# Window attention on one core: VectorE's exponential as a product of factors read from PSUM, GpSimd ungated, lead-in padded

## The chip, the cores and the metric

The kernel runs on one core of one Trainium2 chip. The metric is device time in microseconds (us) of one execution. The profile's span of the same execution is 1.8 us shorter (1096.08 against 1094.3 for the kernel before), so times are compared with times and spans with spans. Five engines count here. TensorE ("PE" in the profile, its weight loads "PEld") multiplies. ScalarE (ACT) takes exponentials out of PSUM, the accumulator memory. VectorE (DVE) does arithmetic and moves results from PSUM to SBUF. GpSimd (POOL) helps with arithmetic, from SBUF alone. SyncE (SP) issues transfers.

## The reference

Cross-shaped window attention on a 224 x 224 image with 96 channels in bfloat16. Half of the channels attend inside horizontal stripes 8 rows high, half inside vertical stripes 8 columns wide. Each stripe has 1,792 positions, and there are 28 of each kind.

```python
qkv = jnp.einsum('bhwc,cd->bhwd', x, wqkv)
q, k, v = qkv[..., :C], qkv[..., C:2 * C], qkv[..., 2 * C:]
scale = C2 ** (-0.5)                                   # C2 = 48
qh = q[..., :C2].reshape(B * nh, sw * W, C2)           # 28 stripes, 1792 positions
... # kh, vh the same
ah = _softmax(jnp.einsum('bqc,bkc->bqk', qh, kh) * scale, axis=-1)
oh = jnp.einsum('bqk,bkc->bqc', ah, vh).reshape(B, H, W, C2)
... # qv, kv, vv, av, ov: the same with vertical stripes and the other 48 channels
return jnp.einsum('bhwc,cd->bhwd', o, wo)
```

The heavy part is the exponential: 56 stripes x 1,792 x 1,792 scores. The kernel cuts them into 1,372 tiles of 128 x 1024.

## The kernel before

The kernel is a program that *plans*: while it emits instructions it keeps a clock of its own for each engine (`now`, `tfree`), with an assumed duration for every instruction, and always gives the next instruction to the engine that would be free. On the chip each engine then runs its fixed list in order, held by semaphores. So a change of one duration or one constant reorders everything that follows it. A score tile goes one of three ways.

On ScalarE, one instruction, assumed to occupy it for 917 ns and to finish after 1277:

```python
e = add("act", [ev, bufA_ev[sl]], lambda e, base=base, sl=sl: e.activation(
    PTA[sl][:], ps[:, base * 512:(base + 2) * 512], ACTF.Exp, scale=LN2 / 128.0), 917.0, 1277.0)
```

On VectorE, by arithmetic: the scores are scaled so that the number, rounded to a 16-bit integer, is nearly the bit pattern of the bfloat16 exponential. What is missing is a correction that depends on the fraction of the exponent, and this fraction can be read as the low half of the 32-bit word. A cubic in it is computed in five passes, the middle three from SBUF to SBUF in 16 bits:

```python
D_OCC = [t_ps(1024), 0.521 * 1024 + 75, 0.26 * 1024 + 75, 0.521 * 1024 + 75, t_ps(1024)]

def d_step(k, sl):
    if k == 0:
        return lambda e: e.tensor_scalar(tt_sb[:], dps.bitcast(U16)[:, 0:2048:2], CS / 65536.0, CS * CA3, ALU.mult, ALU.add)
    if k == 1:
        return lambda e: e.tensor_tensor(sq_sb[:], tt_sb[:], tt_sb[:], ALU.mult)
    if k == 2:
        return lambda e: e.tensor_scalar(sq_sb[:], sq_sb[:], CB, None, ALU.add)
    if k == 3:
        return lambda e: e.tensor_tensor(tt_sb[:], sq_sb[:], tt_sb[:], ALU.mult)
    return lambda e: e.scalar_tensor_tensor(PTD[sl][:].bitcast(U16), dps, CC, tt_sb[:], ALU.add, ALU.add)
```

On GpSimd, after VectorE has copied the tile to SBUF (`zp_sb`), by six operations of the same arithmetic. Each carries a gate, a wait for the instruction that VectorE issued last, and is planned only where VectorE is about to read PSUM; it may be cut into halves of 512 to fit:

```python
gate = (s_dve, cnt["dve"] - 1, 0.0)
c0, c1 = 512 * pick[0], 512 * pick[1]
ev = add("pool", ws + [gate], lambda e: p_step(e, k, zi, sl, c0, c1), p_dur(k, n))
```

The lead-in is written by hand: the first key and query projections, four padding matmuls, the first score tiles, then further projections ("fills"). Transposed input is loaded and results are stored through SyncE's queue.

The softmax here doesn't subtract the row's maximum and nothing guards it: scores larger than these inputs give would overflow.

## Time and profile before

| | before |
|---|---|
| time, median of the first 3 runs | 1095.41 us (1094.14 to 1096.42) |
| span of the profiled run | 1094.3 us, granted TensorE clock 0.993 |
| score tiles on ScalarE / VectorE / GpSimd | 1169 / 158 / 45 |
| busy: ScalarE / VectorE / TensorE / GpSimd | 98% / 96% / 95% / 53% |
| first exponential on ScalarE begins / last one ends | 8.40 / 1088.24 us |

How to read it: all tiles need an exponential, ScalarE takes most of them, and it is hardly ever idle. So the time is the number of ScalarE's tiles times its pace, plus a start, gaps and a tail. The lines are shown in the prediction.

### The profile page before, as it was taken

The numbers are of one execution on the slowest core, as the hardware profiler recorded it, in microseconds if no ns is written. First come the engines' busy times: TensorE is split into PE (matmuls) and PEld (weight loads), VectorE is DVE, ScalarE is ACT, GpSimd is POOL, SyncE is SP. The second block draws the span as 40 slices with busy tenths as digits, with TensorE's granted clock in tenths as the row PEclk, the third lists the DMA queues.
The fourth block names the chain that finished last, engine by engine and source line by source line (L and its number), as shares of the span: only waits on it lengthen the run. The fifth ranks groups of instructions, "written<-read, shape, count | busy, mean of one in ns | idle before, by whom it ended". The sixth has DMA issues, their size and how long they took to land.

```text
span 1094.3 us, 28704 instructions
## 1 busy us (share of the span) xinstructions
PE 1040.7 (95%) x12104; PEld 372.7 (34%) x12104; DVE 1047.4 (96%) x1712; ACT 1077.2 (98%) x1172; POOL 584.6 (53%) x451
## 2 busy tenths in 40 slices
PE   9999999999999999999999999999999999999997
PEld 2333333332333333233333333333333333333332
DVE  5999999999999999999999999999999999999996
ACT  6999999999999999999999999999999999999997
POOL 0544555453545645364564465656565565656563
PEclk7999999999999999999999999999999999999999
DMA  5301001101110120110111122122222222221111
GB/s 99 69 9 35 19 18 36 36 10 27 36 27 10 35 36 7 30 35 17 20 35 27 35 44 41 39 41 42 41 41 40 39 42 41 39 41 38 24 28 37
DMA packets 169001, 37.37 MB, mean 34 GB/s; under 512 B 168872, under 2 KB 168872, under 8 KB 168872
## 3 DMA queue, kind: packets, MB, share of 16 engines
q1 hardware_dynamic: 167256, 35.35, 17.3%
q8 instruction: 94, 1.54, 0.6%
q10 hardware_dynamic: 1616, 0.18, 0.1%
q14 instruction: 35, 0.29, 0.1%
HBM read 0.15 MB, written 9.63 MB: 9 GB/s over the span
## 4 chain that ended last, share of the span: by engine, by line
ACT 71%; DVE 21%; PE 4%; POOL 1%; issue 1%; DMA 0%; SPq 0%; DVEq 0%; POOLq 0%
ACT PTA L892 71%; DVE tt_sb L903 4%; DVE PTD L910 3%; DVE sq_sb L905 2%; DVE tt_sb L909 2%; PE ps L194 2%; PE ps L853 1%; DVE sq_sb L907 1%; DVE KT_sb L522 1%; DVE zp_sb L1056 1%; DVE tmp L624 1%; DVE OT_sb L937 1%; DVE V_sb L431 1%; POOL PTP L985 1%; DVE QT_sb L498 1%
## 5 line engine op out<-in xcount | busy, mean ns | idle before, releaser
L892 ACT ACTIVATE PTA<-ps 128x1024 bf16<-128x1024 f32 x1169 | 1075.0, 1214 | 5.9 <-PE ps L194 5.1
L194 PE MATMUL ps<-QT_sb,KT_sb 49*64 49x512 bf16 (+3 forms) x5488 | 486.5, 369 | 38.9 <-ACT PTA L892 25.5
L853 PE MATMUL ps<-PTA,V_sb 128*64 128x512 bf16 (+1 forms) x2674 | 422.9, 367 | 0.6 <-DVE Ph_sb L584 0.2
L190 PEld LDWEIGHTS <-KT_sb 49*64 49x64 bf16 (+1 forms) x5488 | 137.4, 103 | 335.0 <-issue 321.9
L903 DVE TENSOR_SCALAR tt_sb<-ps 128x1024 f16<-128x1024 uint16 x158 | 192.9, 1221 | 11.6 <-PE ps L194 7.1
L910 DVE SCALAR_TENSOR_TENSOR PTD<-ps,tt_sb 128x1024 uint16<-128x1024 f32 x158 | 192.5, 1219 | 1.3
L853 PEld LDWEIGHTS ps<-PTA,V_sb 128*64 128x64 bf16 x2674 | 119.8, 108 | 204.1 <-issue 162.8
L647 POOL TENSOR_TENSOR out_sb<-tmp,Ph_sb 128x480 bf16<-128x480 f32 (+2 forms) x89 | 105.6, 1195 | 110.9 <-DVE sq_sb L907 57.9
L978 POOL TENSOR_TENSOR uq_sb<-up_sb 128x1024 f16<-128x1024 f16 (+1 forms) x52 | 101.3, 1952 | 111.6 <-DVE sq_sb L907 57.5
L982 POOL TENSOR_TENSOR up_sb<-uq_sb,up_sb 128x512 f16<-128x512 f16 (+1 forms) x65 | 112.3, 1732 | 84.8 <-DVE sq_sb L907 27.4
L984 POOL TENSOR_TENSOR zp_sb<-zp_sb,up_sb 128x512 f32<-128x512 f32 (+1 forms) x74 | 111.2, 1508 | 54.6 <-DVE sq_sb L907 31.7
L976 POOL TENSOR_SCALAR up_sb<-zp_sb 128x1024 f16<-128x1024 uint16 x45 | 47.1, 1047 | 130.3 <-DVE zp_sb L1056 115.4
L905 DVE TENSOR_TENSOR sq_sb<-tt_sb 128x1024 f16<-128x1024 f16 x158 | 113.1, 716 | 0.1
L909 DVE TENSOR_TENSOR tt_sb<-sq_sb,tt_sb 128x1024 f16<-128x1024 f16 x158 | 109.9, 696 | 2.9
L462 PE MATMUL ps<-xT_sb,w_sb 128*64 128x448 bf16 (+3 forms) x448 | 85.7, 380 | 6.1 <-DVE KT_sb L522 3.0
L937 DVE CAST OT_sb<-ps 128x512 bf16<-128x512 f32 (+5 forms) x118 | 69.3, 591 | 1.4 <-PE ps L853 1.4
L907 DVE TENSOR_SCALAR sq_sb<-sq_sb 128x1024 f16<-128x1024 f16 x158 | 68.2, 432 | 2.2
L1056 DVE COPY zp_sb<-ps 128x1024 f32<-128x1024 f32 x45 | 55.0, 1222 | 8.8 <-POOL PTP L985 4.6
L853 PE MATMUL ps<-PTD,V_sb 128*64 128x512 bf16 (+1 forms) x360 | 62.1, 362 | 0.0
L985 POOL TENSOR_SCALAR PTP<-zp_sb 128x512 uint16<-128x512 f32 (+1 forms) x66 | 57.4, 870 | 5.7 <-POOL zp_sb L984 0.2
L624 DVE TENSOR_TENSOR tmp<-ps,rc 128x480 f32<-128x480 f32 (+2 forms) x92 | 53.2, 578 | 1.1
L522 DVE TENSOR_TENSOR KT_sb<-ps,shift 128x448 bf16<-128x448 f32 (+2 forms) x84 | 51.6, 615 | 2.1 <-PE ps L462 2.1
(55 smaller groups left out, 668.3 us busy)
## 6 DMA issues: line engine op xcount, KB each, us to landing
out_dram<-out_sb SPq DMA_DIRECT2D x389, 24.0 KB, 1.9
xT_sb<-in_x_dram SPq DMA_TRANSPOSE x332, 2.6
w_sb<-in_wqkv_dram ACTq DMA_DIRECT2D x2, 54.0 KB, 3.1
out_dram<-out_sb ACTq DMA_DIRECT2D x3, 24.0 KB, 1.9
wo_sb<-in_wo_dram SPq DMA_DIRECT2D x4, 9.0 KB
wo_sb<-one_sb SPq DMA_DIRECT2D x4, 0.0 KB
```

Source lines behind the costliest of these rows:

```text
L190: return e.add_instruction(mybir.InstLdweights(tile_size=(64, 64), tile_position=pos, name=nc.get_next_instruction_name(), engine=mybir.En ...
L194: return e.add_instruction(mybir.InstMatmult(start_tensor_calc=True, stop_tensor_calc=True, tile_size=(64, 64), tile_position=pos, ldweigh ...
L647: return e.tensor_tensor(out_sb[b][:, wdw, k0:k0 + n, :], tmpi[:, 0:n, :], Ph_sb[:, k0:k0 + n, j, :], ALU.add)
L853: ins = e.matmul(bk[64 * wdw:64 * wdw + 64, 0:qs], lhsT=V_sb[b][:, wdw, kt, :], rhs=pt[:, wdw * 512 + i * qs:wdw * 512 + (i + 1) * qs], st ...
L892: e = add("act", [ev, bufA_ev[sl]], lambda e, base=base, sl=sl: e.activation(PTA[sl][:], ps[:, base * 512:(base + 2) * 512], ACTF.Exp, sca ...
L903: return lambda e: e.tensor_scalar(tt_sb[:], dps.bitcast(U16)[:, 0:2048:2], CS / 65536.0, CS * CA3, ALU.mult, ALU.add)
L905: return lambda e: e.tensor_tensor(sq_sb[:], tt_sb[:], tt_sb[:], ALU.mult)
L909: return lambda e: e.tensor_tensor(tt_sb[:], sq_sb[:], tt_sb[:], ALU.mult)
L910: return lambda e: e.scalar_tensor_tensor(PTD[sl][:].bitcast(U16), dps, CC, tt_sb[:], ALU.add, ALU.add)
L978: return e.tensor_tensor(q, u, u, ALU.mult)
L982: return e.tensor_tensor(u, q, u, ALU.mult)
L984: return e.tensor_tensor(z, z, u, ALU.add)
```

## The change

Its intent is to give ScalarE fewer tiles by using GpSimd's idle half. VectorE's correction is rewritten as a product of three linear factors of the fraction, each read from PSUM anew, so that no pass of it should need the SBUF ports that VectorE shares with GpSimd. GpSimd then needs no gates and no halves, and takes 94 tiles. The key projection's shift loses its SBUF pass in the same manner. The lead-in gets eight more padding matmuls, against the fall of TensorE's clock. The planner's constants are chosen anew.

```diff
-CS, CA3, CB, CC = 2.153502696265075, 0.9658066371188914, -31.056571874438696, 55.5867689628946
+CD, CA, CB = 9.864582734494235, 2.9538561147169977, -3.956077288180509
+PS, PA, PB, PC = 2.153502696265075, 0.9658066371188914, -31.056571874438696, 55.5867689628946
 ... (NZP 1 -> 2, SLACK 120 -> 160, LOOK 8 -> 7, HOLD 0 -> 110, ENDD, PADA = 5, PADB = 1, and other planner constants)
-        D_OCC = [t_ps(1024), 0.521 * 1024 + 75, 0.26 * 1024 + 75, 0.521 * 1024 + 75, t_ps(1024)]
+        D_OCC = [t_ps(1024)] * 4
+        HA = CA / 2
+        RT = (HA * HA - CB) ** 0.5
         def d_step(k, sl):
+            frac = dps.bitcast(U16)[:, 0:2048:2]
             if k == 0:
-                return lambda e: e.tensor_scalar(tt_sb[:], dps.bitcast(U16)[:, 0:2048:2], CS / 65536.0, CS * CA3, ALU.mult, ALU.add)
+                return lambda e: e.tensor_scalar(tt_sb[:], frac, (HA + RT) * U, CD / U ** 3, ALU.add, ALU.mult)
             if k == 1:
-                return lambda e: e.tensor_tensor(sq_sb[:], tt_sb[:], tt_sb[:], ALU.mult)
+                return lambda e: e.scalar_tensor_tensor(sq_sb[:], frac, (HA - RT) * U, tt_sb[:], ALU.add, ALU.mult)
             if k == 2:
-                return lambda e: e.tensor_scalar(sq_sb[:], sq_sb[:], CB, None, ALU.add)
-            if k == 3:
-                return lambda e: e.tensor_tensor(tt_sb[:], sq_sb[:], tt_sb[:], ALU.mult)
-            return lambda e: e.scalar_tensor_tensor(PTD[sl][:].bitcast(U16), dps, CC, tt_sb[:], ALU.add, ALU.add)
+                return lambda e: e.tensor_tensor(tt_sb[:], sq_sb[:], frac, ALU.mult)
+            return lambda e: e.tensor_tensor(PTD[sl][:].bitcast(U16), tt_sb[:], dps, ALU.add)
 ... (GpSimd: whole tiles, no safe(), no gate)
-                ev = add("pool", ws + [gate], lambda e: p_step(e, k, zi, sl, c0, c1), p_dur(k, n))
+                ev = add("pool", ws, lambda e: p_step(e, k, zi, sl), p_dur(k))
 ... (K's shift: the SBUF pass becomes a second pass from PSUM)
 ... (lead-in)
+        pad(PADA)
         early_qk(2)
+        for f in [pf0["K"][1], pf0["V"][0]]:
+            f.run_now()
+        early_qk(3)
         for f in [pf0["V"][1], pf0["K"][2]]:
             f.run_now()
-        early_qk(3)
+        pad(PADB)
+        early_qk(4)
         for f in [pf0["V"][2], pf0["K"][3]]:
             f.run_now()
+            pad(PADB)
```

## The prediction

> **What bounds the kernel now.** I read the page first, then the waits of ScalarE, then the timelines of the start, the middle and the end. Every one of the 1,372 score tiles (128x1024) needs an exponential. Part 5 of the page tells who computes it: 1,169 on ScalarE (line 892), 158 on VectorE (one pass each of lines 903, 905, 907, 909, 910), 45 copied out by VectorE (line 1056) and computed on GpSimd (lines 976 to 985); 1169 + 158 + 45 = 1372.
>
> ```profile
> PE 1040.7 (95%) x12104; PEld 372.7 (34%) x12104; DVE 1047.4 (96%) x1712; ACT 1077.2 (98%) x1172; POOL 584.6 (53%) x451
> L892 ACT ACTIVATE PTA<-ps 128x1024 bf16<-128x1024 f32 x1169 | 1075.0, 1214 | 5.9 <-PE ps L194 5.1
> L903 DVE TENSOR_SCALAR tt_sb<-ps 128x1024 f16<-128x1024 uint16 x158 | 192.9, 1221 | 11.6 <-PE ps L194 7.1
> L905 DVE TENSOR_TENSOR sq_sb<-tt_sb 128x1024 f16<-128x1024 f16 x158 | 113.1, 716 | 0.1
> L909 DVE TENSOR_TENSOR tt_sb<-sq_sb,tt_sb 128x1024 f16<-128x1024 f16 x158 | 109.9, 696 | 2.9
> L907 DVE TENSOR_SCALAR sq_sb<-sq_sb 128x1024 f16<-128x1024 f16 x158 | 68.2, 432 | 2.2
> ```
>
> ScalarE's exponentials overlap (1214 ns each by record), so their cost is the busy time over the count, 1075.0 / 1169 = 0.920 us. The reader should see the idle time in the second line: 5.9 us in the whole run. The timeline of ScalarE says where it lies.
>
> ```profile
> 8.40 1.94 ACT L892 ACTIVATE PTA<-ps 128x1024 bf16<-128x1024 f32 x2 [1.03 <-PE ps L194]
> ...
> 16.88 1.02 ACT L892 ACTIVATE PTA<-ps 128x1024 bf16<-128x1024 f32 x1 [0.54 <-PE ps L194]
> 18.44 1.02 ACT L892 ACTIVATE PTA<-ps 128x1024 bf16<-128x1024 f32 x1 [0.54 <-PE ps L194]
> 20.00 1.02 ACT L892 ACTIVATE PTA<-ps 128x1024 bf16<-128x1024 f32 x1 [0.54 <-PE ps L194]
> ...
> 99.46 973.82 ACT L892 ACTIVATE PTA<-ps 128x1024 bf16<-128x1024 f32 x1059
> ```
>
> From 24.4 us on ScalarE is without a gap, but for one of 0.18 us: 1,059 exponentials run as one block. So the span is: start to first exponential, 8.4; 1169 x 0.920 = 1075; gaps after the first exponential, 4.9 - of which the nine between 8.4 and 24.4 us sum to 3.9; and the tail after the last exponential (end at 1077.10 + 11.14 = 1088.24) of 6.1. That makes 1094.4 against a span of 1094.3. ScalarE is the bound; VectorE at 96% is almost one, and GpSimd has 47% idle.
>
> The nine early gaps have one cause. The windows view shows TensorE's clock falling to half at 11 us and staying there until 24:
>
> ```profile
> 10.00:11.00 1.00, 1.00 (x26) 0.69 (x23) 1.00 (x2) 0.69 (x2) 0.00 (x0) 1.00 0.35 54
> 11.00:12.00 1.00, 1.00 (x10) 0.27 (x9) 1.00 (x3) 0.69 (x2) 0.00 (x0) 0.54 0.45 92
> ...
> 22.00:24.00 2.00, 2.00 (x14) 0.44 (x12) 1.68 (x3) 1.39 (x2) 0.00 (x0) 0.50 0.54 104
> 24.00:26.00 2.00, 2.00 (x26) 0.64 (x22) 0.86 (x5) 1.53 (x2) 0.00 (x0) 0.82 0.49 83
> ```
>
> (Length, then busy time and count of PE, PEld, DVE, ACT, POOL, then the clock.) The score matmuls then come too late, and a lone exponential costs 1.02 instead of 0.92.
>
> **Why GpSimd is half idle.** Its timeline beside VectorE's:
>
> ```profile
> 337.58 2.44 POOL L982 TENSOR_TENSOR up_sb<-uq_sb,up_sb 128x1024 f16<-128x1024 f16 x1 [2.97 <-DVE QT_sb L494]
> 337.35 0.68 DVE L909 TENSOR_TENSOR tt_sb<-sq_sb,tt_sb 128x1024 f16<-128x1024 f16 x1
> ...
> 678.48 2.13 POOL L984 TENSOR_TENSOR zp_sb<-zp_sb,up_sb 128x1024 f32<-128x1024 f32 x1
> ```
>
> The bracket is the gate that the kernel puts on GpSimd: it may start only where VectorE is about to make a PSUM pass. Even so it was 0.45 us late at the end of VectorE's pass 909, and the operation reads 2.44. I laid each full-width two-input operation of GpSimd over VectorE's passes: those that begin 0.45 us before the end of a pass 909 are 0.31 longer than clean ones, those 0.58 before it are 0.44 longer, and 2.43 - 0.31, 2.56 - 0.44 and the clean 2.12 of line 984 agree. The square of line 978 (same operand twice) gives 2.20 - 0.31 = 2.33 - 0.44 = 1.89. One-input operations are 1.05 always.
>
> **What the Trainium skill says.** "SBUF — State Buffer", section "SBUF: two separate sides": VectorE and GpSimd share a port pair, held exclusively for a whole instruction by whichever starts first, on VectorE's side by passes in a two-port mode or with two SBUF inputs. The 0.31 and 0.44 above agree. "VectorE: DVE Perf Modes", "The perf-mode tier table": an operand in PSUM costs VectorE its fast modes. The trace agrees: 1.22 for passes that read PSUM against 0.70 and 0.43 for 16-bit SBUF ones; and the PSUM passes stay at 1.22 while GpSimd runs (line 910 under the operation at 337.58). "GPSIMD Engine Reference", section 3.1, has 2.6 cycles an element for a two-input operation at 1.2 GHz, an estimate of 2.2 us for 1,024; the trace has 2.12. "TensorE: Matmul & The Clock Gate", Part 1: the clock halves after an idle window of about 3.4 us and comes back after a busy one. The trace shows the halving, but at half clock for 13.6 us with PE written as busy all through, so the record's busy time is not the activity that counts.
>
> **The change, part by part.** The order of the changed kernel's instructions counts 1,161 exponentials on ScalarE, 117 tiles on VectorE, 94 on GpSimd.
>
> ScalarE: 8 exponentials fewer, 8 x 0.920 = 7.4 us off the path. That is the only sure gain.
>
> VectorE: a tile loses three SBUF passes (0.70 + 0.43 + 0.72) and gets four PSUM passes. Start to start, a PSUM pass takes 1.13 (line 903 at 298.82, the next instruction at 299.95), an SBUF one 0.72, 0.34 or 0.61 where it isn't held. So a tile was 1.13 + 0.72 + 0.34 + 0.61 + 1.13 = 3.93 and becomes 4 x 1.13 = 4.52. In sum 158 x 3.93 = 621 becomes 117 x 4.52 = 529; copies go from 45 x 1.14 = 51 to 94 x 1.14 = 107; K's shift swaps 27 passes of 0.45 and 28 small ones of 0.21 for 27 of 0.62, about -1. Net -37: busy 1047 becomes about 1010, 93%. VectorE gets slack; no gain by itself.
>
> GpSimd: a tile is 3 x 1.05 + 1.89 + 2 x 2.12 = 9.28, plus six gaps of 0.09 between dependent operations (312.52 after an end at 312.43): 9.8. 94 x 9.8 = 921. The 89 additions of line 647 cost 52 x 1.10 + 26 x 0.91 + 11 x 0.55 = 87, plus gaps of 0.09, 95. Sum 1016 of about 1060 that it has between 27 us and the end: 96%. It just fits, off the path. The schedule was laid with 2.13 for all three two-input operations, so the square gives 94 x 0.24 = 22 us of reserve.
>
> Lead-in: 12 padding matmuls instead of 4, five of them where PE now idles (8.6 to 9.5 us). If the clock holds, the nine gaps (3.9) and nine restarts (0.1 each) go, 4.8 at most; I take 3.8, for some gaps stay, since PE must still wait for x and for evacuations. If the clock falls anyway, 0. K's first chunk gets a second PSUM pass (0.69) for a small pass and an SBUF one (0.21 + 0.35): the first exponential comes 0.1 later. I give the clock 70%: -0.7 x 3.8 + 0.1 = -2.6.
>
> Tail: VectorE tiles may now come up to the second tile from the end; in the changed order one more VectorE tile lies in the last stretch, but its PSUM passes end before the final evacuation, so 0.
>
> Sum: -7.4 - 2.6 + 0 = -10.0. From 1095.4: 1085.4; I write 1085.5.
>
> **Rivals.** First, GpSimd becomes the bound. At 96% it has 40 us; if two-input operations took 2.44, as many do now, that is 94 x 2 x 0.32 + 94 x 0.3 = 88 us more, and the time would be about 1130. Against it: what lengthens them is VectorE's SBUF passes, and none is left after the start. Second, ScalarE starves because VectorE's tiles, now four dependent passes, or late GpSimd tiles hold up PE, which issues in order; 1% of starvation is 11 us and would eat the gain (1096). For it: PE and all others run one fixed order that was planned with assumed durations. Against: those (1.14 for PSUM passes) match the trace, and the same planner left ScalarE without gaps before. Third, the clock still falls in the lead-in: 1088.
>
> **Range and chances.** Clock held and nothing starved gives 1084 to 1085, clock lost 1088, light starvation up to 1094; a mean exponential of 0.917, as in the best stretches, would give 1081. So 1081 to 1093. 2% faster would be 1073.5, which needs 23 fewer exponentials: 2%. 2% slower is 1117, the first rival: 4%.
>
> **What would show it.** ScalarE's row: 1,161 exponentials at 0.920 with under 4 us idle; no long wait of it on PE after 30 us. VectorE's four passes 1.22 each, busy near 93%. GpSimd's rows 1.05, 1.89, 2.12, busy near 95%. The clock at 1.0 from 11 to 24 us. Wrong would be: GpSimd operations over 2.3, waits of PE on GpSimd's tiles, gaps of ScalarE in the middle of the run.

## The result

The kernel after takes 1082.38 us (median of 4 runs, 1082.18 to 1082.79) beside 1094.78 for the kernel before on the same chip in the same rounds. The ratio of the fast runs is 0.9885, with a 95% interval of 0.9868 to 0.9902. Such a ratio is the mean time of one kernel's fast runs over that of the other's of the same rounds, so it is not quite the ratio of the medians that are quoted. The result is within 2%, on the fast side. All four runs had a clock of 0.999 or 1.0.

First the page of the kernel after: busy time by engine, then groups of instructions (busy us, mean ns of one, idle time before them and what ended it).

```profile
PE 1030.4 (95%) x12065; PEld 374.3 (35%) x12065; DVE 1025.8 (95%) x1411; ACT 1066.9 (99%) x1164; POOL 959.3 (89%) x662
L892 ACT ACTIVATE PTA<-ps 128x1024 bf16<-128x1024 f32 x1161 | 1064.7, 1290 | 1.9 <-PE ps L198 1.9
L911 DVE TENSOR_SCALAR tt_sb<-ps 128x1024 f32<-128x1024 uint16 x117 | 142.8, 1221 | 11.1 <-PE ps L198 6.6
L915 DVE TENSOR_TENSOR tt_sb<-sq_sb,ps 128x1024 f32<-128x1024 f32 x117 | 141.6, 1210 | 0.1
L985 POOL TENSOR_TENSOR uq_sb<-up_sb 128x1024 f16<-128x1024 f16 x94 | 178.1, 1894 | 7.3
L989 POOL TENSOR_TENSOR up_sb<-uq_sb,up_sb 128x1024 f16<-128x1024 f16 x94 | 200.2, 2130 | 7.0
```

ScalarE has 1,161 exponentials and 1.9 us of idle time before them, of 1,169 and 5.9. VectorE's passes take 1.21 to 1.22 us each although GpSimd now runs through most of the span beside them, and GpSimd's operations have their clean lengths.

ScalarE's timeline in the kernel after (start, length, instruction, and in brackets the idle time before it):

```profile
9.34 3.79 ACT L892 ACTIVATE PTA<-ps 128x1024 bf16<-128x1024 f32 x4 [1.17 <-PE ps L198]
13.45 1.02 ACT L892 ACTIVATE PTA<-ps 128x1024 bf16<-128x1024 f32 x1 [0.33 <-PE ps L198]
14.86 15.83 ACT L892 ACTIVATE PTA<-ps 128x1024 bf16<-128x1024 f32 x17 [0.39 <-PE ps L198]
...
99.01 975.77 ACT L892 ACTIVATE PTA<-ps 128x1024 bf16<-128x1024 f32 x1064
```

Nine gaps between 8.4 and 24.4 us have become two, and the windows view (same columns as in the prediction) shows the clock at full where it stood at half:

```profile
11.00:12.00 1.00, 1.00 (x21) 0.51 (x17) 0.59 (x1) 1.00 (x2) 0.00 (x0) 1.00 0.27 46
22.00:24.00 2.00, 2.00 (x24) 0.59 (x20) 2.00 (x3) 2.00 (x3) 0.00 (x0) 1.00 0.49 105
```

The chain that ended last, by engine. Before:

```profile
ACT 71%; DVE 21%; PE 4%; POOL 1%; issue 1%; DMA 0%; SPq 0%; DVEq 0%; POOLq 0%
```

After:

```profile
ACT 97%; SPq 1%; PE 0%; DMA 0%; DVE 0%; issue 0%
```

In the kernel before a fifth of the chain ran over VectorE, although ScalarE's idle column had only 5.9 us. In the kernel after it is ScalarE's from end to end.

**Where the 13.3 us of span came from.** Idle time tells only a part of it, because exponentials overlap in the record: in a queue one is written with 1.2 to 1.3 us while the next has begun. What tells is the distance between the *ends* of consecutive ones. Its median is 917 ns in both kernels, and its least 913. This count is worked out from both traces, from 30 us on:

```
distance of ends, ns      up to 930   930 to 1000   over 1000   sum over 917
before (1,151 of them)       1125           9           17        3.2 us
after  (1,139 of them)       1139           0            0        0.1 us
```

The sum for the two profiled runs:

| | before | after | difference, us |
|---|---|---|---|
| first exponential begins | 8.40 | 9.34 | +0.9 |
| exponentials x 0.917 | 1169 | 1161 | -7.3 |
| lateness over 917 ns, up to 30 us (lead-in) | 5.2 | 1.1 | -4.1 |
| lateness over 917 ns, after 30 us | 3.2 | 0.1 | -3.1 |
| tail after the last exponential | 6.1 | 6.2 | +0.1 |

That makes -13.5 against a measured 1081.0 - 1094.3 = -13.3. The +0.9 is chance, not the change: the kernel begins with 14 warm-up matmuls, which took 4.68 us in the one run and 5.66 in the other, and in both the first exponential began 2.5 us after their end (8.40 after 5.90, and 9.34 after 6.88). Other profiled kernels with the same start have 4.5 to 6.2 us there.

One of the 26 late exponentials, from the kernel before (timeline, the end is 1,149 ns after the one before it):

```profile
670.34 2.53 POOL L647 TENSOR_TENSOR out_sb<-tmp,Ph_sb 128x480 bf16<-128x480 f32 x2 [3.32 <-DVE KT_sb L506]
672.03 0.97 DVE L513 TENSOR_SCALAR KT_sb<-KT_sb,shift 128x448 bf16<-128x448 bf16 x1
...
676.84 0.38 PE L462 MATMUL ps<-xT_sb,w_sb 128*64 128x448 bf16 x2 [0.24 <-DVE KT_sb L522]
```

Read it from the top. VectorE's pass over K (line 513, from SBUF to SBUF) takes 0.97 us, where its median is 0.33, and it overlaps an addition of GpSimd that runs until 672.87. VectorE's list is full, so the 0.65 us lost are handed on. TensorE stands before a projection matmul until VectorE has emptied a bank (line 522), and the next score matmuls, which lie behind it in TensorE's list, begin at 677.16.

Counted over the whole trace: of the 502 SBUF passes of lines 905, 907, 909 and 513, 33 took at least 0.12 us longer than the shortest of their line. Of the 26 late exponentials 21 end within 7.2 us after the start of such a held pass, and the other five within 5 us after one of these 21. Of all exponentials after 30 us only 19% end so soon after a held pass. The change removes the passes of all four lines.

The theory that the experiments have to test has three parts: the count of tiles, the clock in the lead-in, and lateness in the middle that the shared ports made. Its main rival is that the lead-in and the planner's new constants did most of it.

### The profile page after: what moved, and what is told of

It is laid out like the page before. It is cut to its first block, busy times and chain, and to the rows that moved or that the text cites. A ratio compares the mean times of both kernels' runs of the same rounds, so it can differ in the third digit from the quotient of the medians.

```text
span 1081.0 us, 28395 instructions
## 1 busy us (share of the span) xinstructions
PE 1030.4 (95%) x12065; PEld 374.3 (35%) x12065; DVE 1025.8 (95%) x1411; ACT 1066.9 (99%) x1164; POOL 959.3 (89%) x662
## 3 DMA queue, kind: packets, MB, share of 16 engines
q1 hardware_dynamic: 167256, 35.35, 17.1%
## 4 chain that ended last, share of the span: by engine, by line
ACT 97%; SPq 1%; PE 0%; DMA 0%; DVE 0%; issue 0%
ACT PTA L892 97%; SPq L205 1%; DMA xT_sb<-in_x_dram 0%; PE ps L853 0%; PE ps L198 0%; DVE tmp L624 0%; DVE out_sb L647 0%; PE ps L612 0%; PE ps L1176 0%; DVE OT_sb L943 0%; PE ps L467 0%; DVE rc L618 0%; PE ps L724 0%
## 5 line engine op out<-in xcount | busy, mean ns | idle before, releaser
L892 ACT ACTIVATE PTA<-ps 128x1024 bf16<-128x1024 f32 x1161 | 1064.7, 1290 | 1.9 <-PE ps L198 1.9
L989 POOL TENSOR_TENSOR up_sb<-uq_sb,up_sb 128x1024 f16<-128x1024 f16 x94 | 200.2, 2130 | 7.0
L991 POOL TENSOR_TENSOR zp_sb<-zp_sb,up_sb 128x1024 f32<-128x1024 f32 x94 | 200.5, 2133 | 6.3
L985 POOL TENSOR_TENSOR uq_sb<-up_sb 128x1024 f16<-128x1024 f16 x94 | 178.1, 1894 | 7.3
L911 DVE TENSOR_SCALAR tt_sb<-ps 128x1024 f32<-128x1024 uint16 x117 | 142.8, 1221 | 11.1 <-PE ps L198 6.6
L983 POOL TENSOR_SCALAR up_sb<-zp_sb 128x1024 f16<-128x1024 uint16 x94 | 98.4, 1047 | 54.2 <-DVE zp_sb L1033 47.7
L913 DVE SCALAR_TENSOR_TENSOR sq_sb<-ps,tt_sb 128x1024 f32<-128x1024 uint16 x117 | 142.1, 1214 | 0.2
L916 DVE TENSOR_TENSOR PTD<-tt_sb,ps 128x1024 uint16<-128x1024 f32 x117 | 141.6, 1211 | 0.4
L915 DVE TENSOR_TENSOR tt_sb<-sq_sb,ps 128x1024 f32<-128x1024 f32 x117 | 141.6, 1210 | 0.1
L1033 DVE COPY zp_sb<-ps 128x1024 f32<-128x1024 f32 x94 | 114.9, 1223 | 18.6 <-PE ps L198 14.2
L987 POOL TENSOR_SCALAR uq_sb<-uq_sb 128x1024 f16<-128x1024 f16 x94 | 98.4, 1047 | 8.2
L992 POOL TENSOR_SCALAR PTP<-zp_sb 128x1024 uint16<-128x1024 f32 x94 | 98.4, 1047 | 8.2
L492 DVE SCALAR_TENSOR_TENSOR KT_sb<-ksum,ps 128x448 bf16<-128x448 f32 (+1 forms) x112 | 68.7, 613 | 3.6 <-PE ps L467 2.7
```

The lines of the kernel that those rows point to most:

```text
L911: return lambda e: e.tensor_scalar(tt_sb[:], frac, (HA + RT) * U, CD / U ** 3, ALU.add, ALU.mult)
L913: return lambda e: e.scalar_tensor_tensor(sq_sb[:], frac, (HA - RT) * U, tt_sb[:], ALU.add, ALU.mult)
L915: return lambda e: e.tensor_tensor(tt_sb[:], sq_sb[:], frac, ALU.mult)
L916: return lambda e: e.tensor_tensor(PTD[sl][:].bitcast(U16), tt_sb[:], dps, ALU.add)
L985: return e.tensor_tensor(q, u, u, ALU.mult)
L989: return e.tensor_tensor(u, q, u, ALU.mult)
```

## The experiments

Medians are given, then the ratio of fast runs to the kernel before with its 95% interval where it matters. Lateness means the sum over 917 ns as above. A run that is more than 1.5% slower than the fastest of its kernel counts as slow and stays out of ratios.

### e1_no_pads: the kernel after without the eight new padding matmuls

```diff
-    PADA = 5
-    PADB = 1
+    PADA = 0
+    PADB = 0
```

> The changed kernel with the padding matmuls of the lead-in taken out (5 and 3 of 12; the first 4, which the kernel before has too, stay). 1162 exponentials on ScalarE instead of 1161. Theory (the padding keeps TensorE's clock up, and the clock is what made the early gaps): the clock record shows half speed for 3 to 14 us somewhere between 9 and 25 us, ScalarE idles 3 to 5 us after its first exponential instead of 0.7, and the time is 1085.5 to 1088 against 1082.4 of the changed kernel. Rival (the new order of the lead-in, with the third score tile ahead of K's second chunk, did it and the padding is idle work): idle under 1.5 us, time 1082 to 1084.

Measured: 1085.28 us, from four runs: 1101.04 (clock 0.976, slow), 1082.61 (0.999), 1085.17 and 1085.38 (0.994). The plan comes out with 1,162 exponentials. A windows line of the slow, profiled run:

```profile
12.00:13.00 1.00, 1.00 (x14) 0.51 (x14) 1.00 (x3) 1.00 (x2) 0.00 (x0) 0.50 0.41 88
```

Without pads the clock is lost in three runs of four. Losing it in the lead-in costs 1085.3 - 1082.6 = 2.7 us, two runs against one; that is just under the 1085.5 where the expected range began. In one run the clock held by chance, and that run is as quick as the padded kernel. The slow run lost the clock near the end as well, and nothing is built on it.

### e2_before_pads: the kernel before with the lead-in of after, planned anew (a miss)

```diff
+    PADA = 5
+    PADB = 1
-                return 4 + rr[0] % 4
+                return 5 + rr[0] % 3
 ... (bank 3 -> bank 4 in pad(), and the lead-in's order as in the change)
```

> The kernel before with the changed kernel's lead-in only (order of the first fills, banks, padding). Its schedule comes out with 1171 exponentials on ScalarE, 2 more than before. Theory: the clock holds, the early gaps of 3.9 us shrink to 1 or less, restarts save 0.9, two exponentials cost 1.8: net -2 to -3.5 us, so 1091 to 1093; the late exponentials in the middle of the run (3 us more than 917 ns each) stay. Rival (the lead-in carries more of the gain): under 1089.

Measured: 1115.83 us (1115.45 to 1117.16), ratio 1.0196. The lead-in did what was expected: two gaps, of 0.32 and 0.38 us. But the planner, started from another moment, laid a worse schedule behind it, with 1,171 exponentials on ScalarE, 40 tiles on GpSimd, 24 us of lateness after 30 us, and a clock of 0.977 to 0.98 in all four runs:

```profile
261.70 1.94 ACT L894 ACTIVATE PTA<-ps 128x1024 bf16<-128x1024 f32 x2 [4.79 <-PE ps L855]
```

Here ScalarE waits 4.79 us for the matmuls that consume its results, with all its output buffers full. So this run says nothing of the lead-in, except that such a kernel must be changed *after* planning if one part is to be tested.

### e5_pads_same_plan: five pads put into the kernel before, the plan untouched

```diff
+        for _ in range(5):
+            ops["pe"].append(([e_warm], lambda e: e.matmul(bank(4)[:, :], lhsT=warm[:, 0:128], rhs=warm[:, :], start=True, stop=True), False))
         for f in [pf0["K"][1], pf0["V"][0]]:
```

> The kernel before with five padding matmuls put behind the second score tile (where TensorE idles 0.9 us), outside of the planner's books, so that every other instruction keeps its place; 1169 exponentials as before. It replaces the failed test of the lead-in, whose plan had changed. Theory (idle TensorE time there is what loses the clock): clock 0.998 or more in all or nearly all runs and 1091 to 1093, as the runs of the kernel before that kept their clock by luck (1091.3 and 1092.7 at 0.999, against 1094.9 to 1096.5 at 0.992 to 0.994). Rival (five pads are too few, or the fall has another cause): clocks spread as before.

Measured: 1092.01 us (1091.59 to 1092.57), clock 0.998 or 0.999 in all four runs. The kernel before in the same rounds has 1091.5 to 1091.6 in three runs that kept the clock and 1094.5 to 1096.0 in four that did not; ratio 0.9981 (0.9959 to 1.0003).

```profile
11.09 49.72 ACT L892 ACTIVATE PTA<-ps 128x1024 bf16<-128x1024 f32 x54 [0.49 <-PE ps L194]
```

From 11.09 us ScalarE runs without a gap. The lateness after 30 us stays, 3.0 us. So pads buy certainty, the quick kind of run each time: four of four here, three of seven without them. Against the median of the kernel before in the same rounds they are worth 1094.5 - 1092.0 = 2.5 us, though the interval of the ratio just includes 1, and against its own lucky runs nothing. The rest of the gain, 1092.0 - 1082.4 = 9.6, is something else.

### e4_p45: the kernel after with GpSimd held to 45 tiles

```diff
-    NPT = 400
+    NPT = 45
```

> The changed kernel with GpSimd limited to 45 tiles, as before. The planner gives 1192 exponentials to ScalarE and 135 tiles to VectorE. Theory (the time is the start, 917 ns for each exponential of ScalarE, and the end): 1082.4 + 31 x 0.917 = 1110.8, so 1109 to 1113, slower than the kernel before. Rival (VectorE's near-saturation sets the time, and fewer copies relieve it): well under 1105.

Measured: 1111.61 us (1111.24 to 1113.07), ratio 1.0158 (1.0133 to 1.0182). GpSimd is 46% busy, VectorE has 135 tiles, and the exponentials end 917 ns apart:

```profile
L892 ACT ACTIVATE PTA<-ps 128x1024 bf16<-128x1024 f32 x1192 | 1093.1, 1304 | 2.4 <-PE ps L198 2.4
```

31 more of them than in the kernel after are 31 x 0.917 = 28.4 us, and 1082.4 + 28.4 = 1110.8. The 49 tiles that GpSimd gains are thus what pays. The rewritten exponential, the padded lead-in and the new constants without them lose against the kernel before; the constants weren't chosen anew for 45 tiles.

### e3_lock: one VectorE pass gets two SBUF inputs again (wrong factors on purpose)

```diff
-                return lambda e: e.tensor_tensor(tt_sb[:], sq_sb[:], frac, ALU.mult)
+                return lambda e: e.tensor_tensor(tt_sb[:], sq_sb[:], sq_sb[:], ALU.mult)
```

> The changed kernel with one operand of one VectorE pass altered: the third pass multiplies sq_sb by itself instead of by the PSUM fraction, so it has two SBUF inputs. Same instructions, same order, 117 such passes; wrong results on purpose. Theory (a pass with two SBUF inputs and a GpSimd operation exclude each other; freedom from that is what lets GpSimd run ungated): each such pass waits for the rest of a GpSimd operation, about 0.86 us on average (an estimate from 1.05, 1.89 and 2.13 weighted by length) and 88% of the time, so its row shows 1.7 to 2.2 us instead of 1.21, VectorE needs some 90 us more than it has room for, ScalarE is starved in the middle, and the time is 1110 to 1180. Rival (the lock is minor, the gain of ungating is only the missing gate waits): pass under 1.4 us and time under 1090.

Measured: 1204.91 us (1190.55 to 1211.4); two of the four runs count as slow, and the two fast ones took 1190.55 and 1199.61. The order of instructions is that of the kernel after, only one of VectorE's four passes is another. (The correction is small enough that the result still passed.) The row of that pass, which took 1.21 us with one input in PSUM:

```profile
L915 DVE TENSOR_TENSOR tt_sb<-sq_sb 128x1024 f32<-128x1024 f32 x117 | 219.9, 1879 | 0.1
```

GpSimd's one-input operations rise from 1.05 to 1.13, 1.26 and 1.29, its two-input ones from 2.13 to 2.24 and 2.27. Both engines hold each other, and ScalarE pays:

```profile
ACT PTA L892 <- PE ps L198: 76.3, 134, 1.8
```

(Waits of ScalarE on TensorE's scores: us in total, times, longest; a second line of score matmuls adds 17.1.) The range expected ended at 1180. TensorE also lost its clock (0.933 in the profiled run), which had not been counted; that this makes up the rest is likely, not shown.

### e6_before_nogate: the kernel before with GpSimd's gates taken out, the same plan

```diff
-                        fin((s_dve, cnt["dve"] - 1, 0.0))
+                        fin(None)
-                ev = add("pool", ws + [gate], lambda e: p_step(e, k, zi, sl, c0, c1), p_dur(k, n))
+                ev = add("pool", ws, lambda e: p_step(e, k, zi, sl, c0, c1), p_dur(k, n))
```

> The kernel before with the waits of GpSimd on VectorE's progress taken out; plan and order the same, data dependences kept. Theory (the gate keeps GpSimd's operations off VectorE's 16-bit SBUF passes): GpSimd starts its operations earlier and meets more of those passes; VectorE's rows of the three SBUF passes grow from 0.70, 0.43 and 0.72 towards 1 us and more, ScalarE is starved here and there, 1100 to 1140. Rival (the gate only cost waiting): VectorE's rows stay, 1090 to 1095.

Measured: 1345.14 us (1325.68 to 1356.75), of which the two fast runs took 1325.68 and 1339.71; ratio 1.2181, far more than expected.

```profile
L909 DVE TENSOR_TENSOR tt_sb<-sq_sb,tt_sb 128x1024 f16<-128x1024 f16 x158 | 168.7, 1068 | 2.9
L905 DVE TENSOR_TENSOR sq_sb<-tt_sb 128x1024 f16<-128x1024 f16 x158 | 138.2, 875 | 0.1
L907 DVE TENSOR_SCALAR sq_sb<-sq_sb 128x1024 f16<-128x1024 f16 x158 | 99.2, 628 | 2.2
```

These three were 696, 716 and 432 ns with gates. ScalarE waits 192 us for scores and the clock is 0.864 on average in the profiled run. The longer passes alone are 158 x (0.37 + 0.16 + 0.20) = 115 us of VectorE's time, and VectorE was 96% full before. The other half of some 238 us (fast runs against the median of 1094.5) was not taken apart; the expectation had named passes of 1 us and more, but not what they add up to, nor the clock. Ungating and removing the shared-port passes belong together: neither part of the change is a small step by itself.

### e7_before_short_pool: the kernel before with GpSimd's operations made short (wrong result)

```diff
-            z = zp_sb[zi][:, c0:c1]
-            u, q = up_sb[:, c0:c1], uq_sb[:, c0:c1]
+            z = zp_sb[zi][:, c0:c1:(st := 1 if k == 5 else 64)]
+            u, q = up_sb[:, c0:c1:st], uq_sb[:, c0:c1:st]
 ... (k == 0: every 64th element likewise)
```

> The kernel before with GpSimd's first five operations of a tile made 16 elements (8 for a half) instead of 1024 wide, the last kept; plan, order and gates the same; wrong results on purpose. It takes nearly all of GpSimd's hold on the shared ports away and leaves VectorE's passes. Theory (the exponentials that are late in the middle of the run, 3 us over 917 ns each in all, are late because VectorE's SBUF passes wait for GpSimd and TensorE waits for VectorE's evacuations): VectorE's three SBUF passes shrink to about 0.68, 0.42 and 0.68 with none above 0.75, the excess over 917 ns between exponentials after 26 us falls under 0.6 us, the time is about 3 us less than the kernel before at the same clock: 1088 to 1093. Rival (the late ones are in the plan itself, VectorE being full): excess stays at 2.5 to 3.5 us.

Measured: 1092.75 us (1091.9 to 1093.51), clock 0.993 to 0.996, relative error 0.063 as intended. All four runs lost the clock in the lead-in; beside the runs of the kernel before that had lost it in the same rounds (1094.5 to 1096.0) they are 1 to 4 us quicker. The lateness after 30 us falls from 3.2 to 0.65 us, with no instruction moved, just above the 0.6 expected. So four fifths of it came from GpSimd's long operations and went with them, and not from the plan. The chain that ended last is ScalarE's to a larger part (71% before):

```profile
ACT 91%; DVE 5%; PE 4%; issue 0%
```

VectorE's SBUF passes shorten only a little in the mean (716, 696 and 432 ns become 696, 691 and 422), and, other than expected, 14 still take over 0.75 us. A rival is that GpSimd's results and buffers, which come earlier here, had been what VectorE waited for. What is left speaks against it: three late exponentials (over 930 ns), each 6.6 us behind a pass of line 513 that took 0.97 us in place of 0.33. GpSimd's additions of line 647, which hold that pass in the example above, were left long in this run.

### c1_exp_only: the kernel before with the new exponential alone (a miss in size)

```diff
+CD, CA, CB3 = 9.864582734494235, 2.9538561147169977, -3.956077288180509
 ... (D_OCC, d_step as in the change; gates, halves, one zp_sb and the old lead-in kept)
 ... (planner constants chosen anew: DPOL 2, SLACK 140, NBA 7, LOOK 9, HOLD 120, SAFE 200 and others)
```

> The kernel before with the three-factor exponential alone: gates and split GpSimd operations kept, old lead-in, planner numbers chosen anew for it: 1187 ScalarE exps (18 more than before), 142 VectorE tiles, 43 GpSimd tiles. Theory (the rewritten exponential costs VectorE more, and pays only because it lets GpSimd run ungated and take 94 tiles; its own gift is the lateness that the shared ports made, 3 us): +18 x 0.917 = +16.5, -3, so about 1105 us with the clock kept in the lead-in, 1109 with it lost; 1100 to 1112. Rival (the rewritten exponential carries the gain by itself): under 1095 us.

Measured: 1117.99 us (1115.58 to 1120.06), ratio 1.021 (1.0182 to 1.0239), 6 us above the range. The sign of the theory holds: alone, the new exponential is a loss. The profiled run kept its clock in the lead-in; what was not foreseen lies in the middle:

```profile
745.00:750.00 5.00, 3.89 (x61) 1.85 (x59) 4.95 (x7) 5.00 (x6) 3.11 (x3) 1.00 0.18 36
752.00:754.00 2.00, 2.00 (x17) 0.73 (x15) 1.58 (x3) 1.43 (x2) 0.64 (x2) 0.50 0.23 45
992.00:996.00 4.00, 4.00 (x24) 0.89 (x24) 2.48 (x3) 2.30 (x4) 2.98 (x2) 0.50 0.20 38
```

TensorE was busy for 3.89 of 5 us, then its clock fell to half, near 750 and near 990 us. These two places gave 6.6 us of lateness, other late exponentials 2.4, and without these 9.0 the profiled run would have had 1115.6 - 9.0 = 1106.6, against the 1105 that the theory had for a kept clock and no lateness. Whether another choice of constants would avoid the two falls was not tried.

### b1_quadratic: a cheaper correction, fitted to what bounds the kernel now

If only ScalarE's count matters, shorter tiles on the two helpers are what to look for. A quadratic correction (the error of the fit is 0.17%) needs three VectorE passes in place of four and four GpSimd operations in place of six.

```diff
-                return lambda e: e.tensor_scalar(tt_sb[:], frac, (HA + RT) * U, CD / U ** 3, ALU.add, ALU.mult)
+                return lambda e: e.tensor_scalar(tt_sb[:], frac, -QR1 * U, QC / U ** 2, ALU.add, ALU.mult)
             if k == 1:
-                return lambda e: e.scalar_tensor_tensor(sq_sb[:], frac, (HA - RT) * U, tt_sb[:], ALU.add, ALU.mult)
-            if k == 2:
-                return lambda e: e.tensor_tensor(tt_sb[:], sq_sb[:], frac, ALU.mult)
-            return lambda e: e.tensor_tensor(PTD[sl][:].bitcast(U16), tt_sb[:], dps, ALU.add)
+                return lambda e: e.scalar_tensor_tensor(sq_sb[:], frac, -QR2 * U, tt_sb[:], ALU.add, ALU.mult)
+            return lambda e: e.tensor_tensor(PTD[sl][:].bitcast(U16), sq_sb[:], dps, ALU.add)
 ... (GpSimd the same with PN = 4; some planner constants)
```

> A version meant to beat both: the correction of the exponential is a quadratic (error 0.17 per cent by the fit, below the step of bf16) instead of a cubic, so VectorE has three PSUM passes a tile and GpSimd four operations (1.05, 1.89, 2.13, 1.05); some of the planner's numbers were re-chosen. The plan gives 1109 exponentials to ScalarE, 126 tiles to VectorE, 137 to GpSimd. Theory (time = start, 917 ns a ScalarE exponential, end): 1082.4 - 52 x 0.917 = 1034.7, so 1033 to 1040 if nothing starves. VectorE's busy time 95%, GpSimd's about 90%. Rival (TensorE, 95% busy by record, is the next bound and cannot go faster): above 1060, with late score tiles all through.

Measured: correct, 1054.89 us (1046.7 to 1059.16), ratio 0.9629 (0.9572 to 0.9686). 1,109 exponentials stay on ScalarE, 126 tiles go to VectorE and 137 to GpSimd. That misses the 1033 to 1040 expected. Up to 900 us the exponentials end 917 ns apart, so TensorE, the rival, does not bound them; after it 18.6 us of lateness come in two places, from 932 and from 969 us. GpSimd's timeline at the second:

```profile
968.95 1.09 POOL L647 TENSOR_TENSOR out_sb<-tmp,Ph_sb 128x480 bf16<-128x480 f32 x1 [6.73 <-DMA out_dram<-out_sb]
```

An addition of GpSimd waits 6.73 us for an output transfer (there are two such waits, 13.0 us together) out of the buffer that it is to fill: there are two such buffers, and SyncE issues the transfers behind input transposes. VectorE, TensorE and ScalarE then follow, and the clock falls.

### b2_quadratic_out3: a third output buffer

```diff
-        out_sb = [sb(f"out_sb{i}", [128, 2, NKT, C], BF16) for i in range(2)]
+        out_sb = [sb(f"out_sb{i}", [128, 2, NKT, C], BF16) for i in range(3)]
 ... (semaphores and uses: index b -> P % 3)
```

> The quadratic-correction kernel with three output buffers in place of two, TensorE's order unchanged, 1109 ScalarE exps. Theory (its stall at 926 to 994 us came from GpSimd's last addition waiting for the output transfer, 6.7 us, whose buffer was still being sent): those waits are gone, the exponentials stay 917 ns apart to the end, the clock is kept, and the time is 1082.4 - 52 x 0.917 = 1034.7, so 1034 to 1040 us. Rival (another wait of VectorE or GpSimd takes its place in the same stretch, because VectorE and GpSimd are both nearly full there): over 1045 us.

Measured: 1047.27 us (1045.83 to 1049.48), ratio 0.9564 (0.9539 to 0.959). The theory was right as to the stall, for the exponentials end 917 ns apart to the last, with 0.2 us of lateness after 30 us. But the time missed its range, since the tail after the last exponential has grown from 6.2 to 19.4 us. SyncE's queue says why:

```profile
909.76 20.33 SPq L206 DMA_DIRECT2D out_dram<-out_sb  x28
930.19 21.88 SPq L205 DMA_TRANSPOSE xT_sb<-in_x_dram  x16
952.12 93.12 SPq L206 DMA_DIRECT2D out_dram<-out_sb  x136
```

From 577 us on it issues almost without a pause, in turns of 28 output transfers and 16 transposes, about 20 and 22 us a turn, and ends with 136 transfers in 93.12 us, 0.68 each. Neither the rival nor the theory had named this: an engine that no busy row of the page lists had become the bound of the end. The chain of waits put only 1% on it.

### b3_quadratic_x4: a fourth buffer for the transposed input

```diff
-    NXB = 3
+    NXB = 4
-        E_W = (s_w, w_tot[0], 0.0)
+        E_W = (s_w, w_tot[0], 0.0) if plan_x_load(3, []) is None else None
```

The order on the four computing engines is the same; on SyncE 16 transposes move from the second half to the first, where that queue has time.

> b2_quadratic_out3 with a fourth buffer for the transposed input, so that the input transposes of every pass are issued one pass earlier; order on the four computing engines unchanged. In b2_quadratic_out3 the last exponential ends 19.4 us before the end (6.2 in the kernel after), and SyncE's queue issues without a pause from 577 us on: 28 output transfers x 0.69 and 16 transposes x 1.37 us per pass of about 41 us. Theory (SyncE's issuing is the bound of that tail): 16 transposes, 21.9 us, move to the front, where that queue waits anyhow; the tail goes back to about 6.2 us, so 1047.3 - 13.2 = 1034.1, within 1032 to 1038. Rival (what holds the output is the transfers themselves, or GpSimd that makes their data late): 1043 to 1048 us, the tail near 19 us still.

Measured: correct, 1036.32 us (1035.44 to 1036.54, five runs, clock 0.998 or 0.999), ratio 0.9473 (0.9448 to 0.9498). The rival is out.

```profile
884.95 21.59 SPq L205 DMA_TRANSPOSE xT_sb<-in_x_dram  x16
906.59 125.97 SPq L206 DMA_DIRECT2D out_dram<-out_sb  x164
```

SyncE's last transposes end at 906.54 in place of 952.07 us. The queue now waits 20 us for GpSimd's additions (4 before), the tail is 7.2 us, and this kernel beats the kernel after by 1082.4 - 1036.3 = 46.1 us. 52 fewer exponentials account for 52 x 0.917 = 47.7, of which a tail that is 1.0 longer takes some back.

## Why the prediction was right

The time, 1082.38 us, lies in the range of 1081 to 1093, and in the class held the likeliest, but 3.1 us under the predicted 1085.5. The lower end of the range was there for a mean of 0.917, without the reason why it would come; so that the time fell inside is in part luck. By its own steps:

- *"8 exponentials fewer, 8 x 0.920 = 7.4 us off the path. That is the only sure gain."* Right: 1,161 were counted, worth 7.3, and e4_p45 shows the rate in another size, 28.4 us for 31. But it was not the only sure gain.
- *The mean exponential of 0.920.* This is the step that was mis-sized. The prediction took 0.920 as what an exponential costs and carried it into the kernel after, where it is 1064.7 / 1161 = 0.917. The 0.003 x 1169 = 3.0 us above 917 ns were no cost of the operation. By the trace 1.3 of them belong to the lead-in, where twelve exponentials start from an idle engine and take 1.02 us (the prediction has these in its restarts). The other 1.7, with 0.8 us of idle time, are the 26 late exponentials after 30 us. e7_before_short_pool takes four fifths of that lateness away, and e5_pads_same_plan leaves it.
- *"From 24.4 us on ScalarE is without a gap, but for one of 0.18 us."* A misreading behind that step: after 30 us the trace has 14 gaps, 0.8 us in all, and the timeline view joins instructions that lie less than about 0.15 us apart. The clues were in view: of its 4.9 us of gaps the prediction placed only 3.9 and 0.18, and the chain of waits had 21% on VectorE.
- *Lead-in: -0.7 x 3.8 + 0.1.* Right in kind: the clock held in all four runs, and seven of nine gaps went. The lateness in the lead-in fell by 4.1, close to the 3.8 of the case in which the clock holds; the 70% made it 2.6. Weighting was fitting for another reason: the kernel before keeps its clock by luck in a third of its runs, so against its median pads are worth 2.5 (e5_pads_same_plan), and e1_no_pads shows the same lottery in the kernel after. The +0.1 for K's shift can't be seen in the two profiled runs (2.49 and 2.45 us from the end of the warm-up to the first exponential), but the experiments show it: 2.45 or 2.46 us in all six that are built on the kernel after, 2.31 in the four that are built on the kernel before and keep its lead-in.
- *Tail 0.* Right, +0.1.
- *GpSimd "just fits" with rows of 1.05, 1.89 and 2.12.* Right, 1.05, 1.89 and 2.13. Its busy share of 89% is under the 95 to 96% written because the gaps of 0.09 between operations were put into the sum and the page does not count them as busy. The bound was as far off as was said.
- *VectorE near 93%.* It is 95%. The passes go as it said, 1.13 to 1.14 us from start to start (medians). About 7 of the 16 us that were missed come from 176 reciprocals, which the next instruction now no longer overlaps (it begins 0.21 us after their start, where it was 0.15); the prediction left them out of its sum. About as much comes from K's shift, which adds some 6 us where the sum had -1. It cost nothing.
- *Rivals.* The first (GpSimd held by VectorE) is real as a mechanism: e3_lock makes it with one pass, at +108 and +117 us in its fast runs. It did not come because no such pass was left, which is the reason given. The second (starvation) had its sign wrong: a light starvation was in the kernel before, and the change removed it. The third (clock lost) is e1_no_pads.
- *The skill's table of VectorE's modes.* The prediction says a little too much: with an operand in PSUM the table takes the fourfold mode away and still allows a single-source operation up to the twofold. No run here shows such a pass.

The two profiled runs differ by 13.3 us, more than the 9.6 between e5_pads_same_plan and the kernel after, because the profiled run of before was one of those that had lost the clock.

## What to carry to other kernels

When the bounding engine's instructions overlap in the record, measure the distance between their ends against the best stretch, for lateness of up to a tenth of an instruction (917 ns in a queue, 1.02 us from idle) leaves no idle time to be seen. When a resource that two engines share is taken out of one of them, look for the gain in what the other may then do (49 more tiles), and test the two halves together, since each alone was a loss. After each step read the queue of the engine that only issues transfers: it became the bound beside computing engines that were 88% to 97% busy, and two more buffers, without one instruction less, gave 1054.9 - 1036.3 = 18.6 us.

## What the Trainium skill lacked or had wrong

- "TensorE: Matmul & The Clock Gate", Part 1, ties the halved clock to an idle window of about 3.4 us, and the return to a busy one of the same length. Here the clock stayed at half for 13.65 us with TensorE's row full (prediction, 11 to 24 us), and in c1_exp_only it fell after 5 us in which TensorE was busy for 3.89. The same part names short idle times between groups of matmuls as a second way to lose the clock; what share of use loses it isn't on the page, and the row of busy time does not show it. The traces agree with the length of the window: all stretches at half clock but a run's last are multiples of 3.41 us (13.65 here, 6.83 in e7_before_short_pool). That it varies from run to run the page says of the warm-up; here it decides 3 to 4 us of a long kernel, in 21 of 32 runs.
- "GPSIMD Engine Reference", section 3.1: 2.6 cycles an element for two inputs (an estimate of 2.2 us for 1,024 elements at 1.2 GHz) against 2.13 measured, so it agrees roughly. Lacking, as times of an instruction: the same tensor given twice costs less, 1.89 us, and an operation with one input 1.05.
- "SBUF — State Buffer", section "SBUF: two separate sides", agrees with e3_lock and e6_before_nogate. Lacking: one tensor given twice to VectorE counts as two SBUF inputs as well (1.21 becomes 1.88 us), and gates on time slots still leave lateness (3.2 us).
- "ScalarE: Activation LUTs", section "What ACT_TABLE_LOAD costs", has 186 + 0.833 N ns for an activation with immediate scale and bias and an overlap of about 93 ns back to back, an estimate of 1039 - 93 = 946 for N = 1,024. Measured: 1.02 us alone, 917 ns from end to end. Lacking there: a queued one is recorded with 1.2 to 1.3 us, so that lateness hides in the record.
- "DMA: Bandwidth & Descriptors", section "Issuing engines are not separate DMA queues", calls the sequencer's time to start a transfer "usually small relative to the DMA itself". Here it was not, and it bounded a kernel: an output transfer of 24 KB took SyncE 0.68 us to issue beside 1.9 us to land, a transpose 1.37 beside 2.6, together about 41 us for each turn of 28 and 16 (b2_quadratic_out3).
